# Start of a two-part kernel: x loaded in whole rows, q's weights in column parts, copies of turned x ahead of index tables

## The chip, the cores and the metric

The kernel runs on one NeuronCore of one Trainium2 chip. The metric is the device time of one execution in microseconds (us). All engine names are those of the profile: PE is TensorE's matmul, PEld its weight load, DVE is VectorE, ACT is ScalarE, POOL is GpSimd, SP is SyncE, which here only issues transfers. SPq, ACTq and POOLq are the queues of instructions that issue transfers or wait.

## The reference

Two computations that share nothing, their outputs set side by side (bf16, 2048 tokens of 576 features each).

```python
# A: attention over a dilated window
qkv = (x @ wqkv)                      # 2048 x 576 by 576 x 1728; 32 heads of 18
idx = pos - 2 * arange(8)             # each token looks at itself and 7 earlier ones
attn = softmax(einsum(q, k[idx]) * scale)        # masked where idx < 0
a = einsum(attn, v[idx]) @ wo
# B: a short convolution, then one as long as the sequence
kv = (sum over t of k_pad shifted by t * shift_k[:, 3 - t]) * v     # 4 taps
y = irfft(rfft(kv) * rfft(ssm_k)) + kv * ssm_D
b = q * y
out = concatenate([a, b], -1)
```

## The kernel before

Everything is written as one function with an order laid down by hand. The PE work that has no fixed place is put in a list of units (projections, spectra of the filter and of kv, output products); the call `until()` pops as many units as the next number of the tuple `PLACES` says, and so sets how many units stand on PE between two steps of the rest. `FKS` and `FXS` set how the units of the filter spectrum (L610, L611, `ps_fk`) and of the kv spectrum (L766, `ps_fx`) are mixed with the projections of v.

The beginning, with which the change deals, runs as follows.

* **x** (2048 tokens) is needed turned, features on partitions, in blocks kb of 128 features. Its first two quarters of 512 tokens (qtr 0 and 1) are loaded as they are (L179) and turned on PE (L450, 128x128 each; L455 for the last 64 features) into the PSUM tiles `ps_x`. The other two quarters come turned by the transfer itself (L236).
* **The load** of a quarter puts token 128 sb + p on partition p as its row sb: four separate rows of 576 features (1152 bytes) per partition.
* **The copies** of the turned quarter 0 from PSUM to `xw`: blocks 0 and 1 by DVE (L510), 2 and 3 by ACT (L511), the tail of 64 features by ACT (L460). Quarter 1 is copied by ACT alone, two blocks at a time (L521).
* **q's weights** come with `load_w(nc.sync, 0)`: one transfer for the first 512 rows (L139), two for the last 64, the tails (L141), all from SP's queue, behind x's first quarter and ahead of its second.
* **The index tables**: `table_k(0)`, `table_k(1)`, `table_x(0)`, `table_x(1)` each are two DVE multiply-adds (L421) and one mask (L422) in int32; ACT later takes their sine (L423). Two tables stand ahead of DVE's copies and two behind.
* **The taps' factors** `shift_k` are spread over the partitions by PE (`spread_taps`, L496, into `ps_sk`) and copied to `skb` by ACT (L499); the piece 256 to 511 is spread between the turning of quarter 0 and the first projection.
* **The first projection** `project_first(jp, ct0)` (L483, L485) makes two column tiles of q for 512 tokens: all four blocks for the first tile (e = 0), then all four for the second, then both tails. It runs for (0, 0), (0, 2), (1, 0), (1, 2), with the turning of quarter 1 after the first. Other projections (L363 and on) follow as units.
* DVE then multiplies the taps of kv for four blocks of 512 tokens (`taps`, L560, L564, L580), which takes it to 54.7 us; `negate` (L636) makes a row that `fold_filter` needs, and `fold_filter` (PE L650, ACT L653) overwrites the row that `negate` read. The logits' products (DVE L822), their sums on PE (L837, `ps_log`) and the eviction of those (ACT L842) follow, then the softmax (L865 to L882).

`Ks` holds x as loaded (`xnat`) and the tables (`n_all`) at first, later the filter. `pp` gives PSUM banks in two tags, A and B, two of each.

Of the kernel before, what the change touches and what calls it, by code (L numbers as in the profile page):

```python
# [11 lines left out]
ACT = mybir.ActivationFunctionType  # L12
ALU = mybir.AluOpType
FP32 = mybir.dt.float32
BF16 = mybir.dt.bfloat16
I32 = mybir.dt.int32
PSUM = bass.MemoryType.PSUM

PLACES = (
    15, 4, 11, 2, 1, 0, 3, 4, 6, 4, 13, 4, 4, 0, 4, 3, 4, 2, 1, 3, 4, 3, 5, 5, 0, 7, 2, 2, 2, 1, 2, 2, 2, 2, 3,  # L20
    1, 0, 3, 2, 0, 8, 3, 0, 1, 12, 1, 1, 0,
)

FKS = (
    3, 1, 0, 0, 0, 0, 0, 0, 0, 0, 0, 0, 0, 0, 0, 0, 0, 0, 1, 0, 0, 0, 0, 2, 0, 0, 2, 0, 0, 0,
)
FXS = (
    7, 2, 0, 12, 13, 2, 0, 0, 4,
)

EARLY = (
# [8 lines left out]
def view(t, offset, dims):  # L40

    return bass.AP(tensor=t.tensor, offset=t.offset + offset, ap=[list(t.ap[0])] + [list(d) for d in dims])
# [3 lines left out]
def kernel(  # L46
# [13 lines left out]
    nc = tc.nc  # L60
    Bsz, S, D = A_x.shape
# [3 lines left out]
    xf = A_x.flatten_outer_dims()  # L65
# [23 lines left out]
    HB = 4 * D  # L89
# [4 lines left out]
    main = ctx.enter_context(tc.tile_pool(name="main", bufs=1))  # L94
# [9 lines left out]
    def bank2(name, tag):  # L104
        return pp.tile([128, 2, 512], FP32, name=name, tag=tag)
# [6 lines left out]
    xw = main.tile([128, 12 * HB], BF16, name="xw")  # L112
# [11 lines left out]
    def xT(kb, t0, n):  # L124
        return view(xw, HB * (3 + 3 * (t0 // 1024)) + 1024 * kb + t0 % 1024, [[1, n]])

    def x5(jj):
        return view(xw, HB * (3 + 3 * jj) + 4096, [[1, 512]])

    def w_at(kb, comp):  # L130
        return HB * (9, 10, 5)[comp] + D * kb if kb < 4 else 11 * HB + D * (1, 2, 0)[comp]

    def wq(kb, comp, c0, n):
        return view(xw, w_at(kb, comp) + c0, [[1, n]])

    def load_w(eng, comp, to=None):
        low, high = (to[:, 0:4, :], to[:, 4, :]) if to is not None else \
            (view(xw, w_at(0, comp), [[D, 4], [1, D]]), wq(4, comp, 0, D))
        eng.dma_start(low, A_wqkv[0:512, comp * D:(comp + 1) * D].rearrange("(kb p) a -> p kb a", p=128))  # L139
        for r in range(2):  # L140
            eng.dma_start(high[64 * r:64 * r + 64, :], A_wqkv[512:576, comp * D:(comp + 1) * D])  # L141

    s1 = ExitStack()
    sp1 = s1.enter_context(tc.tile_pool(name="s1", bufs=1, reuse_waits="tile"))
# [4 lines left out]
    tB = sp1.tile([128, 8 * D], BF16, name="tB")  # L149
    skrow = tB[0:97, 0:4 * D]  # L150
    nc.scalar.dma_start(skrow[96:97, :], B_shift_k.rearrange("d j -> (d j)").unsqueeze(0))
    warm = sp1.tile([128, 1], FP32, name="warm")
    nc.scalar.activation(warm[:], pib[:], ACT.Sin)
    ones96 = sp1.tile([97, 256], BF16, name="ones96")
# [9 lines left out]

    idle_work(4)

    Ks = main.tile([128, 12 * HB], BF16, name="Ks")
    xnat = view(Ks, 4 * HB, [[HB, 4], [D, 4], [1, D]])
    n_all = view(Ks, 8 * HB, [[1, 4 * HB]]).bitcast(I32).rearrange("p (n f) -> p n f", n=9)

    def k_at(m, part):
        return 3 * HB * (3 - m) + HB * part

    def kTok(m):
        return view(Ks, k_at(m, 2), [[D, 4], [1, D]])
    kjs, vts = [], []

    def load_x(qtr):
        nc.sync.dma_start(xnat[:, qtr], xf[512 * qtr:512 * qtr + 512, :].rearrange("(sb p) c -> p sb c", p=128))  # L179

    load_x(0)

    def load_k(i):

        eng = nc.sync
        kj = sp1.tile([128, 7, D], BF16, name="kj", bufs=2)
        r0 = BL * i
        low = [(0, 64)]
        if i == 0:
            nc.gpsimd.memset(kj[0:1, 0:3, :], 0.0)  # L190
            nc.gpsimd.dma_start(kj[0:1, 3:7, :], kf[0:4, :].unsqueeze(0))
            low = [(1, 49), (49, 64)]
        for a, b in ((3, 7), (0, 3)) if i == 0 else ((0, 7),):
# [32 lines left out]
    nc.gpsimd.affine_select(ident[:], ones128[:], pattern=[[1, 128]], compare_op=ALU.is_equal, fill=0.0,  # L226
                            base=0, channel_multiplier=-1)

    load_w(nc.sync, 0)
    load_x(1)  # L230

    def turn_x(h):
# [3 lines left out]
        nc.sync.dma_start_transpose(view(xw, 6 * HB + 512 * h, [[1024, 4], [1, 512]]), xf[r0:r0 + 512, 0:512])  # L236

    load_k(0)
    load_w(nc.sync, 1)
    load_v(0)  # L240
    load_k(1)
    turn_x(0)
# [17 lines left out]
    for h in range(2):  # L260
        f = fold[:, 64 * h:64 * h + 64]
# [39 lines left out]
    q, k = qk[:, 0:4 * S + 1024], qk[:, 4 * S + 1024:]  # L301
# [123 lines left out]
    def table_k(c):  # L425
        return table(n_all[:, 2 * c:2 * c + 2, :], TK[:, c, :, :], n_all[:, 8, :], (2 + c, 2 + c), 2048, (256.0, 1792.0))

    def table_x(n):
        return table(n_all[:, 4 + 2 * n:6 + 2 * n, :], TX[:, 2 * n:2 * n + 2, :], n_all[:, 8, :], (4, 5), 4096,
              (512.0 + 1024.0 * n,) * 2)  # L430
# [22 lines left out]
    def tail_x(qtr, pt):  # L453
        for sb in range(4):
            nc.tensor.transpose(pt[64 * qtr:64 * qtr + 64, 0, 512 + 128 * sb:640 + 128 * sb],  # L455
                                xnat[:, qtr, sb, 512:576], ident[:], tile_position=(0, 64 * qtr))

    def copy_tail(qtr, pt):
        r = slice(64 * qtr, 64 * qtr + 64)
        nc.scalar.activation(x5(0)[r], pt[r, 0, 512:1024], ACT.Copy)  # L460

    def pair_x():
        return pp.tile([128, 2, 1024], BF16, name="ps_x", tag="B")
# [13 lines left out]
    def project_first(jp, ct0):  # L477

        ps = bank2("ps_proj", "A")
        for e in range(2):  # L480
            c0 = 128 * (ct0 + e)
            for kb in range(4):
                nc.tensor.matmul(ps[:, e, :], wq(kb, 0, c0, 128), xT(kb, 512 * jp, 512), start=(kb == 0), stop=False)  # L483
        for e in range(2):
            nc.tensor.matmul(ps[:, e, :], wq(4, 0, 128 * (ct0 + e), 128)[64 * jp:64 * jp + 64],  # L485
                             x5(0)[64 * jp:64 * jp + 64], start=False, stop=True, tile_position=(64 * jp, 0))
        nc.scalar.activation(view(q, S * ct0 + 512 * jp, [[S, 2], [1, 512]]), ps[:], ACT.Copy)
# [13 lines left out]

    spread_taps(512)
    spread_taps(0)
    sines = [table_k(0), table_k(1)]
    pts = [pair_x() for _ in range(2)]
    for n in range(2):
        transpose_x(0, pts[n], 2 * n, range(4))
    tail_x(0, pts[1])
    for n in range(2):
        nc.vector.tensor_copy(xT(n, 0, 512), pts[0][:, n, 0:512])  # L510
        nc.scalar.activation(xT(2 + n, 0, 512), pts[1][:, n, 0:512], ACT.Copy)  # L511
    copy_tail(0, pts[1])
    spread_taps(256)
    sines += [table_x(0), table_x(1)]
    project_first(0, 0)
    pts = [pair_x() for _ in range(2)]
    for n in range(2):
        transpose_x(1, pts[n], 2 * n, range(4))
    tail_x(1, pts[0])
    for n in range(2):  # L520
        nc.scalar.activation(view(xw, 3 * HB + 2048 * n + 512, [[1024, 2], [1, 512]]), pts[n][:, :, 0:512], ACT.Copy)  # L521
    copy_tail(1, pts[0])
    project_first(0, 2)
    sines[2]()
# [185 lines left out]
    raw = view(Ks, k_at(0, 0), [[D, 5], [1, D]])  # L710

    for i in range(NBL):
        r = taps(i)
        if i == 3:
            negate(3, 2)
        until()
        if i < 2:
            load_k(i + 2)
            load_v(i + 2)
        if i == 1:  # L720
            load_filter(0)
            for m in range(1, NBL):
                load_filter(m)
            load_w(nc.sync, 2, raw)
            for m in (3, 2, 1, 0):
                nc.gpsimd.dma_start(other(m), kTok(m)[:, 2, :])
            first_rows()
        if i == 1:
            nc.scalar.preload_act_table_set("natural_log_exp_and_others")
            nc.scalar.activation(warm[:], pib[:], ACT.Exp)  # L730
        mirrors = [(0.5, partial(mirror, i, n), "x") for n in range(2)]
        if i == 2:
            mirrors.append(fold_filter(3))
        if i == 3:
            need("fold3")
            first = made(filter_spectrum, 3)
# [516 lines left out]
    for group in groups:  # L1253
# [50 lines left out]
```

## Time and profile before

| | us |
|---|---|
| median of 3 runs | 213.51 |
| lowest and highest of them | 212.78, 213.68 |
| span of the profiled execution | 211.5 |
| PE busy in it | 200.9 (95%) |
| DVE busy | 197.3 (93%) |
| ACT busy | 151.0 (71%) |

The profiled execution is known by its span alone, from its first instruction to its last, and has no time of its own beside the three runs; a run's time also holds what lies around the span. Times in the profile count from the start of the span. A line number L is a line of the kernel. "Idle before, releaser" is how long the engine stood idle just before the instruction and what ended that; a queue's instructions (SPq, ACTq) are not counted as busy. A matmul's end is modelled, its start is recorded.

### The profile page before, as it was taken

The numbers are of one execution on the slowest core, as the hardware profiler recorded it, in microseconds if no ns is written. First come the engines' busy times: TensorE is split into PE (matmuls) and PEld (weight loads), VectorE is DVE, ScalarE is ACT, GpSimd is POOL, SyncE is SP. The second block draws the span as 40 slices with busy tenths as digits, with TensorE's granted clock in tenths as the row PEclk, the third lists the DMA queues.
The fourth block names the chain that finished last, engine by engine and source line by source line (L and its number), as shares of the span: only waits on it lengthen the run. The fifth ranks groups of instructions, "written<-read, shape, count | busy, mean of one in ns | idle before, by whom it ended". The sixth has DMA issues, their size and how long they took to land.

```text
span 211.5 us, 5096 instructions
## 1 busy us (share of the span) xinstructions
PE 200.9 (95%) x2122; PEld 112.5 (53%) x2122; DVE 197.3 (93%) x150; ACT 151.0 (71%) x218; POOL 69.3 (33%) x104
## 2 busy tenths in 40 slices
PE   7999899999879999999999999999999999999891
PEld 2543344445545556563345566765567667676560
DVE  7989999999978999979979999999999999899982
ACT  3799766967797989984378688864487896765640
POOL 8999991023391367220090000004240000202000
PEclk9999999999999999999999999999999999999999
DMA  6999999999092636998999896589993105453034
GB/s 204 297 317 239 248 323 322 183 238 286 8 135 33 87 56 105 187 159 187 226 222 228 141 232 154 103 211 249 209 278 107 60 3 160 123 167 115 3 106 117
DMA packets 34084, 36.12 MB, mean 171 GB/s; under 512 B 17459, under 2 KB 28847, under 8 KB 34062
## 3 DMA queue, kind: packets, MB, share of 16 engines
q1 hardware_dynamic: 26380, 23.11, 43.8%
q0 software_dynamic: 5216, 10.19, 24.8%
q10 hardware_dynamic: 2466, 2.51, 3.6%
q8 instruction: 16, 0.26, 0.5%
q14 instruction: 6, 0.05, 0.1%
HBM read 13.11 MB, written 4.72 MB: 84 GB/s over the span
## 4 chain that ended last, share of the span: by engine, by line
PE 78%; ACT 10%; issue 3%; SPq 2%; DVE 2%; DMA 2%; DVEq 0%; ACTq 0%
PE ps_proj L363 13%; PE ps_z L1126 9%; PE ps_wo L1020 8%; PE ps_acc L964 7%; PE ps_inv L1158 7%; PE ps_fx L766 7%; PE ps_log L837 4%; PE ps_proj L483 4%; PE ps_fk L610 3%; ACT Ks L670 3%; PE ps_proj L374 2%; DMA Ks<-Ks 2%; SPq L212 2%; PE ps_rev L650 1%; PE ps_sk L496 1%
## 5 line engine op out<-in xcount | busy, mean ns | idle before, releaser
L363 PE MATMUL ps_proj<-xw 128*128 128x512 bf16 x160 | 37.5, 380 | 0.5 <-ACT qk L397 0.5
L822 DVE TENSOR_TENSOR av<-qk 128x4096 bf16<-128x4096 bf16 (+1 forms) x16 | 31.5, 2017 | 1.9 <-ACT xw L592 1.9
L363 PEld LDWEIGHTS <-xw 128*128 128x128 bf16 x160 | 14.4, 98 | 20.1 <-issue 4.8
L1139 ACT ACTIVATE av<-ps_z 128x768 bf16<-128x768 f32 x23 | 17.5, 811 | 5.6 <-PE ps_z L1126 5.6
L768 ACT ACTIVATE xw<-ps_fx 128x576 bf16<-128x576 f32 x32 | 18.8, 673 | 2.4 <-PE ps_fx L766 2.4
L397 ACT ACTIVATE qk<-ps_proj 128x1024 bf16<-128x1024 f32 x14 | 14.3, 1025 | 8.3 <-PE ps_proj L374 4.7
L670 ACT ACTIVATE Ks<-ps_fk 128x576 bf16<-128x576 f32 x32 | 19.0, 688 | 1.1 <-PE ps_fk L611 1.0
L1098 DVE TENSOR_TENSOR qk<-xw,Ks 128x2304 bf16<-128x2304 bf16 x14 | 18.6, 1355 | 1.0 <-PE ps_z L1126 0.7
L560 DVE TENSOR_TENSOR tB<-kj,skb 128x4608 bf16<-128x4608 bf16 (+1 forms) x8 | 19.3, 2416 | 0.1
L766 PE MATMUL ps_fx<-xw,TB 128*128 128x288 bf16 x128 | 17.9, 286 | 0.8 <-ACT xw L592 0.7
L1020 PE MATMUL ps_wo<-qk 128*128 128x288 bf16 x128 | 17.9, 287 | 0.0
L610 PE MATMUL ps_fk<-Ks,TB 128*128 128x384 bf16 x62 | 16.4, 326 | 1.2 <-ACT Ks L670 0.9
L1158 PE MATMUL ps_inv<-av,TI 128*128 128x288 bf16 (+1 forms) x112 | 15.6, 292 | 0.6 <-ACT av L1139 0.6
L766 PEld LDWEIGHTS <-TB 128*128 128x128 bf16 x128 | 12.0, 98 | 6.7 <-issue 3.5
L964 PE MATMUL ps_acc<-av,ident 64*64 64x512 bf16 x160 | 15.3, 379 | 0.0
L611 PE MATMUL ps_fk<-Ks,TB 128*128 128x192 bf16 x62 | 15.2, 246 | 0.0
L1087 POOL DMA_DIRECT2D TB<-in_B_q_dram x4 | 3.0, 738 | 36.7 <-DVE v L1098 23.5
L397 ACT ACTIVATE v<-ps_proj 128x1024 bf16<-128x1024 f32 x9 | 9.3, 1043 | 7.8 <-PE ps_proj L363 4.3
L1020 PEld LDWEIGHTS <-qk 128*128 128x128 bf16 x128 | 11.5, 98 | 6.2 <-issue 3.6
L968 ACT ACTIVATE qk<-ps_acc 128x1024 bf16<-128x1024 f32 x8 | 8.2, 1025 | 8.3 <-PE ps_acc L964 8.3
L947 DVE TENSOR_TENSOR av<-Ks,v 128x4096 bf16<-128x4096 bf16 x6 | 13.6, 2285 | 0.1
L1158 PEld LDWEIGHTS <-TI 128*128 128x128 bf16 x112 | 10.5, 98 | 5.6 <-issue 2.7
(194 smaller groups left out, 465.7 us busy)
## 6 DMA issues: line engine op xcount, KB each, us to landing
Ks<-Ks POOLq DMA_DIRECT2D x7, 576.0 KB, 8.3
TB<-av SPq DMA_DIRECT2D x12, 256.0 KB, 4.9
kj<-in_B_k_dram SPq DMA_DIRECT2D x6, 504.0 KB, 6.1
vt<-in_B_v_dram SPq DMA_DIRECT2D x8, 288.0 KB, 5.0
Ks<-av SPq DMA_DIRECT2D x8, 256.0 KB, 6.0
out_dram<-qk ACTq DMA_DIRECT2D x5, 288.0 KB, 3.2
Ks<-in_A_x_dram SPq DMA_DIRECT2D x2, 576.0 KB, 5.2
xw<-in_A_wqkv_dram SPq DMA_DIRECT2D x2, 576.0 KB, 6.0
```

The source lines that it names most:

```text
L363: nc.tensor.matmul(ps[:, jp, :], wq(kb, comp, 128 * ct, 128), xT(kb, 1024 * jj + 512 * jp, 512), **se)
L397: nc.scalar.activation(view(t, o + pad + 1024 * jj, [[512, 2], [1, 512]]), ps[:], ACT.Copy)
L560: dve(2304 * n, lambda: nc.vector.tensor_tensor(to, view(kj, row * D, [[D, n], [D, 4], [1, D]]), view(skb, row * D, [[D, n], [0, 4], [1, D ...
L610: nc.tensor.matmul(o[:, 0:2], w, rhs[:, 0:2], start=start, stop=stop)
L670: nc.scalar.activation(view(Ks, k_at(m, cs ^ (m & 1)) + 96 * gi, [[768, 3], [384, 2], [1, 96]]), acc3(ps), ACT.Copy, scale=(PSG, MSG)[cs][ ...
L766: nc.tensor.matmul(ps[:, pm, 0:HD], TX[:, 2 * pm + c, 128 * gi:128 * gi + 128], kv[:, 2 * c + pm, HD * h:HD * h + HD], start=(c == 0), sto ...
L768: nc.scalar.activation(view(xw, HB * XG[i] + 96 * gi + 1152 * h, [[HB, 2], [384, 3], [1, 96]]), view(ps, 0, [[512, 2], [96, 3], [1, 96]]), ...
L822: return P, at, step, dve(1024 * nj, lambda: nc.vector.tensor_tensor(view(P, at, [[step, 4], [256, nj], [1, 256]]), view(t, o + 256 * hh, ...
L964: nc.tensor.matmul(acc[64 * o:64 * o + 64, h, :], ident[64 * h:64 * h + 64, 64 * h:64 * h + 64], view(P, 256 * u, [[2048, 2], [1, 256]])[6 ...
L1020: nc.tensor.matmul(ps[:, r, 0:HD], oT(hh, j + 2 * r, t)[:, o:o + 128], wo[:, t // 2, t % 2, HD * h:HD * h + HD], start=(t == 0 and h == 0) ...
L1126: nc.tensor.matmul(view(acc[r], 512 * h, [[192, 2], [96, 2], [1, 96]])[o:o + 64], w[64 * h:64 * h + 64, 64 * h:64 * h + 64], pr[64 * h:64 ...
L1158: nc.tensor.matmul(ps[:, c, 0:n], TI[:, sl, pm, 128 * c:128 * c + 128], Yall[:, j % 2, pm, sl, c0:c0 + n], start=(pm == 0 and sl == 0), st ...
```

## The change

* **x**: a quarter is loaded so that partition p holds tokens 4p to 4p + 3, one run of 4608 bytes. The turned blocks then come out of PE with the tokens in the order (sb, p); the copies put them right by reading PSUM with a step (`turned`: p outer, sb inner, so neighbours lie 128 elements apart).
* **q's weights**: the first 512 rows in two transfers, columns 0 to 255 and 256 to 575, on SP right behind x's first quarter; the two tails on ACT's queue, behind `shift_k` and ahead of ACT's first table of functions.
* **Copies**: quarter 0's blocks 0, 1 and 3 by DVE, block 2 by ACT, right behind the first table (`table_k(0)`); the other three tables follow them.
* **First projection**: for each block both column tiles, instead of all blocks of one tile first.
* **Numbers of the order**: three of `PLACES`, one of `FXS`. In the built program the one difference that they make on PE is that two more units of the filter's spectrum stand ahead of the logit sums (L837) that the second eviction L842 ends, and two fewer behind.

The number of instructions is the same on PE, DVE and POOL; ACT has one copy less, which DVE has more, and two transfers more to issue, SP one fewer.

```diff
 PLACES = (
-    15, 4, 11, 2, 1, 0, 3, 4, 6, 4, 13, 4, 4, 0, 4, 3, ...
-    1, 0, 3, 2, 0, 8, 3, 0, 1, 12, 1, 1, 0,
+    15, 4, 11, 2, 1, 0, 3, 4, 6, 6, 11, 4, 4, 0, 4, 3, ...
+    1, 0, 3, 2, 0, 8, 3, 0, 1, 10, 1, 1, 0,
 FXS = (
-    7, 2, 0, 12, 13, 2, 0, 0, 4,
+    7, 4, 0, 12, 13, 2, 0, 0, 4,
...
-    def load_w(eng, comp, to=None):
+    def load_w(comp, to=None, parts=((0, D),), tails=nc.sync):
...
-        eng.dma_start(low, A_wqkv[0:512, comp * D:(comp + 1) * D].rearrange("(kb p) a -> p kb a", p=128))
+        for a, b in parts:
+            nc.sync.dma_start(low[:, :, a:b], A_wqkv[0:512, comp * D + a:comp * D + b].rearrange("(kb p) a -> p kb a", p=128))
         for r in range(2):
-            eng.dma_start(high[64 * r:64 * r + 64, :], A_wqkv[512:576, comp * D:(comp + 1) * D])
+            tails.dma_start(high[64 * r:64 * r + 64, :], A_wqkv[512:576, comp * D:(comp + 1) * D])
...
     def load_x(qtr):
-        nc.sync.dma_start(xnat[:, qtr], xf[512 * qtr:512 * qtr + 512, :].rearrange("(sb p) c -> p sb c", p=128))
+        nc.sync.dma_start(xnat[:, qtr], xf[512 * qtr:512 * qtr + 512, :].rearrange("(p sb) c -> p sb c", p=128))
...
     nc.scalar.dma_start(skrow[96:97, :], B_shift_k.rearrange("d j -> (d j)").unsqueeze(0))
+    load_w(0, parts=((0, 256), (256, D)), tails=nc.scalar)
...
-    load_w(nc.sync, 0)
     load_x(1)
...
+    def turned(ap):
+        return ap.rearrange("q (sb p) -> q p sb", sb=4)
+
     def copy_tail(qtr, pt):
         r = slice(64 * qtr, 64 * qtr + 64)
-        nc.scalar.activation(x5(0)[r], pt[r, 0, 512:1024], ACT.Copy)
+        nc.scalar.activation(x5(0)[r], turned(pt[r, 0, 512:1024]), ACT.Copy)
...
-        for e in range(2):
-            c0 = 128 * (ct0 + e)
-            for kb in range(4):
-                nc.tensor.matmul(ps[:, e, :], wq(kb, 0, c0, 128), xT(kb, 512 * jp, 512), start=(kb == 0), stop=False)
+        for kb in range(4):
+            for e in range(2):
+                nc.tensor.matmul(ps[:, e, :], wq(kb, 0, 128 * (ct0 + e), 128), xT(kb, 512 * jp, 512), start=(kb == 0),
+                                 stop=False)
...
-    sines = [table_k(0), table_k(1)]
+    sines = [table_k(0)]
...
-    for n in range(2):
-        nc.vector.tensor_copy(xT(n, 0, 512), pts[0][:, n, 0:512])
-        nc.scalar.activation(xT(2 + n, 0, 512), pts[1][:, n, 0:512], ACT.Copy)
+    for n in (0, 1, 3):
+        nc.vector.tensor_copy(xT(n, 0, 512), turned(pts[n // 2][:, n % 2, 0:512]))
+    nc.scalar.activation(xT(2, 0, 512), turned(pts[1][:, 0, 0:512]), ACT.Copy)
...
-    sines += [table_x(0), table_x(1)]
+    sines += [table_k(1), table_x(0), table_x(1)]
...
-        nc.scalar.activation(view(xw, 3 * HB + 2048 * n + 512, [[1024, 2], [1, 512]]), pts[n][:, :, 0:512], ACT.Copy)
+        nc.scalar.activation(view(xw, 3 * HB + 2048 * n + 512, [[1024, 2], [4, 128], [1, 4]]),
+                             pts[n][:, :, 0:512].rearrange("q n (sb p) -> q n p sb", sb=4), ACT.Copy)
```

More of the change, by code (lines that the diff above doesn't have):

```diff
@@ L19 @@
 PLACES = (
-    15, 4, 11, 2, 1, 0, 3, 4, 6, 4, 13, 4, 4, 0, 4, 3, 4, 2, 1, 3, 4, 3, 5, 5, 0, 7, 2, 2, 2, 1, 2, 2, 2, 2, 3,
-    1, 0, 3, 2, 0, 8, 3, 0, 1, 12, 1, 1, 0,
+    15, 4, 11, 2, 1, 0, 3, 4, 6, 6, 11, 4, 4, 0, 4, 3, 4, 2, 1, 3, 4, 3, 5, 5, 0, 7, 2, 2, 2, 1, 2, 2, 2, 2, 3,
+    1, 0, 3, 2, 0, 8, 3, 0, 1, 10, 1, 1, 0,
 )
@@ L134, in wq, with load_x @@
         return view(xw, w_at(kb, comp) + c0, [[1, n]])
-    def load_w(eng, comp, to=None):
+    def load_w(comp, to=None, parts=((0, D),), tails=nc.sync):
         low, high = (to[:, 0:4, :], to[:, 4, :]) if to is not None else \
             (view(xw, w_at(0, comp), [[D, 4], [1, D]]), wq(4, comp, 0, D))
-        eng.dma_start(low, A_wqkv[0:512, comp * D:(comp + 1) * D].rearrange("(kb p) a -> p kb a", p=128))
+        for a, b in parts:
+            nc.sync.dma_start(low[:, :, a:b], A_wqkv[0:512, comp * D + a:comp * D + b].rearrange("(kb p) a -> p kb a", p=128))
         for r in range(2):
-            eng.dma_start(high[64 * r:64 * r + 64, :], A_wqkv[512:576, comp * D:(comp + 1) * D])
+            tails.dma_start(high[64 * r:64 * r + 64, :], A_wqkv[512:576, comp * D:(comp + 1) * D])
+    Ks = main.tile([128, 12 * HB], BF16, name="Ks")
+    xnat = view(Ks, 4 * HB, [[HB, 4], [D, 4], [1, D]])
+    n_all = view(Ks, 8 * HB, [[1, 4 * HB]]).bitcast(I32).rearrange("p (n f) -> p n f", n=9)
+    def load_x(qtr):
+        nc.sync.dma_start(xnat[:, qtr], xf[512 * qtr:512 * qtr + 512, :].rearrange("(p sb) c -> p sb c", p=128))
+    load_x(0)
     s1 = ExitStack()
@@ L165 @@
     idle_work(4)
-    Ks = main.tile([128, 12 * HB], BF16, name="Ks")
-    xnat = view(Ks, 4 * HB, [[HB, 4], [D, 4], [1, D]])
-    n_all = view(Ks, 8 * HB, [[1, 4 * HB]]).bitcast(I32).rearrange("p (n f) -> p n f", n=9)
     def k_at(m, part):
@@ L176 @@
     kjs, vts = [], []
-    def load_x(qtr):
-        nc.sync.dma_start(xnat[:, qtr], xf[512 * qtr:512 * qtr + 512, :].rearrange("(sb p) c -> p sb c", p=128))
-    load_x(0)
     def load_k(i):
@@ L238 @@
     load_k(0)
-    load_w(nc.sync, 1)
+    load_w(1)
     load_v(0)
@@ L723 @@
                 load_filter(m)
-            load_w(nc.sync, 2, raw)
+            load_w(2, raw)
             for m in (3, 2, 1, 0):
```

## The prediction

> **What bounds the kernel now.** I read the busy time by stretches first, because the shares over the whole span (TensorE 95%, VectorE 93%) do not say which engine is late where. The columns are the stretch in us, its length, then busy us (and instructions) of TensorE matmuls (PE), weight loads (PEld), VectorE (DVE), ScalarE (ACT), GpSimd, then granted clock, DMA share and GB/s.
>
> ```profile
> 5.30:7.80 2.50, 2.47 (x25) 1.57 (x24) 2.47 (x6) 2.00 (x4) 2.34 (x5) 1.00 1.11 320
> 7.80:20.90 13.10, 13.10 (x72) 5.17 (x72) 12.08 (x13) 11.27 (x14) 12.35 (x21) 1.00 1.15 283
> 20.90:24.00 3.10, 2.55 (x27) 1.27 (x26) 3.06 (x3) 3.10 (x4) 3.04 (x3) 1.00 1.00 203
> 24.00:43.20 19.20, 19.20 (x122) 7.97 (x122) 18.85 (x12) 13.17 (x19) 8.72 (x19) 1.00 1.03 277
> 43.20:53.40 10.20, 10.20 (x88) 4.77 (x88) 10.03 (x7) 7.32 (x10) 2.50 (x4) 1.00 0.98 248
> 53.40:64.00 10.60, 8.45 (x83) 5.30 (x80) 8.81 (x8) 9.48 (x16) 6.96 (x9) 1.00 0.54 76
> 76.00:93.80 17.80, 17.54 (x166) 10.72 (x164) 16.36 (x14) 17.26 (x28) 9.55 (x7) 1.00 0.81 135
> ```
>
> PE is full from 5.3 up to 20.9, and again from 24.0 to 53.4; in 20.9 to 24.0 ACT is full (3.10 of 3.10). From 53.4 to 64.0 neither PE nor DVE is full and ACT is the busiest. From 76.0 to 93.8 ACT has 17.26 of 17.80. So the early stage, which nearly the whole diff edits, is set by PE's own list of matmuls. The chain that ended last, in order of time (start, us, what), says the same for the first 10 us:
>
> ```profile
> 1.27 1.89 PE ps_idle L163 x4
> 3.16 2.13 PE ps_sk L496 x6
> 5.29 1.16 PE ps_x L450 x16
> 6.45 0.34 PE ps_x L455 x4
> 6.79 0.97 PE ps_sk L496 x4
> 7.79 1.91 PE ps_proj L483 x8
> 11.58 1.83 PE ps_proj L483 x8
> ```
>
> Each piece starts where the last ended (1.27 + 1.89 = 3.16, and so on). There is no stretch in which PE stands still for x or for q's weights. The timeline shows the two moments closest to one (start, us, engine, line; in brackets the idle time before and what ended it):
>
> ```profile
> 4.98 1.29 PEld L450 LDWEIGHTS <-Ks 128*128 128x128 bf16 x16 [0.60 <-DMA Ks<-in_A_x_dram]
> 7.76 1.45 PEld L483 LDWEIGHTS <-xw 128*128 128x128 bf16 x8 [0.50 <-issue]
> 9.63 0.11 PEld L485 LDWEIGHTS <-xw 64*128 64x128 bf16 x2 [0.42 <-issue]
> ```
>
> The first transposes' weight load does wait for x, until 4.98, but the matmuls before it end at 5.29. The first projection's load starts after 0.50 of idle where a like change of group (L485) has 0.42.
>
> **The change, part by part.** The sum is made against the span, 211.5. The median of the runs shown is 213.51, 2.0 above it, which I take to lie around the span and to stay.
>
> *x and q's weights earlier.* What can be won here is PE waiting, and the chain has 0.03 (7.76 to 7.79) and 0.08 (first projection group 1.91, a later one 1.83): **-0.11** at most. Both fit the copies of turned x, not the loads: DVE makes the copies at 7.23, behind two index tables.
>
> ```profile
> 1.86 1.22 SPq L141 DMA_DIRECT2D xw<-in_A_wqkv_dram  x2
> 1.40 1.28 ACT L153 ACT_TABLE_LOAD   x1 [1.40 <-PEq L1288]
> 3.62 0.39 ACT L499 ACTIVATE skb<-ps_sk 128x256 bf16<-128x256 f32 x1 [0.72 <-PE ps_sk L496]
> ```
>
> ```profile
> xw<-in_A_wqkv_dram SPq DMA_DIRECT2D x1, 576.0 KB, 5.6
> ```
>
> The last row is the transfers of the first 8 us (KB each, us to landing): q's weights, issued ahead of the tails' 1.86, are in before 7.46, ahead of the 7.76 at which PE loads them. In two column parts the runs of memory get shorter (512 and 640 bytes for 1152) and x's longer (4608 for 1152), and no row prices that. The first part has the place in the queue of the whole and half its bytes; the second is first used by the group at 11.58. Below, nothing can be won past the 0.11; above, 0.2 of cover for the first part and some 4 for the second take it in: nothing.
>
> SP loses two issues (1.22) and gains one (some 0.5), so x's second quarter and k follow about 0.7 earlier. ACT's queue gets the two tail loads, 1.22 ahead of its table load: 1.40 + 1.22 + 1.28 = 3.90, and the eviction of 3.62 moves to about 4.1. It frees the bank of the second eight transposes, at about 5.9: nothing. The Trainium skill, "DMA: Bandwidth & Descriptors", section "Issuing engines are not separate DMA queues", holds that starting transfers from several engines saves only the issue time; by it the sum is unchanged.
>
> *Copies ahead of the tables.* In the built order of the changed kernel DVE does one table, three copies (blocks 0, 1, 3), then three tables; ACT copies block 2 and waits for the third DVE copy, a wait that is new. Behind it on ACT stand the tail copy and the last eviction of the spread taps, for which PE's tails and DVE's first tap wait. DVE today:
>
> ```profile
> 4.13 0.88 DVE L421 TENSOR_SCALAR Ks<-Ks,rp 128x512 int32<-128x512 int32 x2
> 5.66 0.93 DVE L421 TENSOR_SCALAR Ks<-Ks,rp 128x512 int32<-128x512 int32 x2
> 7.23 0.75 DVE L510 COPY xw<-ps_x 128x512 bf16<-128x512 bf16 x2
> 11.96 1.36 DVE L560 TENSOR_TENSOR xw<-kj,skb 128x2304 bf16<-128x2304 bf16 x1 [0.82 <-DMA kj<-in_B_k_dram]
> ```
>
> A table is 1.57 (5.66 to 7.23). The new copies read PSUM with a step, which no DVE row of this kernel does. Bounds, from groups kept apart by form (busy, mean ns):
>
> ```profile
> L510 DVE COPY xw<-ps_x 128x512 bf16<-128x512 bf16 x2 | 0.7, 414 | 0.0
> L899 DVE COPY xw<-Ks 128x576 bf16<-128x576 bf16 x1 | 1.2, 1211 | 0.0
> L1167 DVE TENSOR_TENSOR TB<-ps_back,TB 128x384 bf16<-128x384 f32 x2 | 1.0, 552 | 0.8 <-PE ps_back L1185 0.8
> L1167 DVE TENSOR_TENSOR TB<-ps_back,TB 128x768 bf16<-128x768 f32 x1 | 0.9, 950 | 0.0
> L442 ACT ACTIVATE TI<-ps_ti 128x512 bf16<-128x512 f32 x4 | 2.2, 598 | 0.7 <-PE ps_ti L438 0.7
> L511 ACT ACTIVATE xw<-ps_x 128x512 bf16<-128x512 bf16 x2 | 1.1, 596 | 0.5 <-PE ps_x L455 0.5
> ```
>
> At best 414 ns, as now; at worst 1211/576 = 2.1 ns an element as in the stepped SBUF copy L899, 1.08 us. I take the PSUM rows at one element a time: (950 - 552)/384 = 1.04 ns an element, 552 + 128 x 1.04 = **0.685**. The Trainium skill, "VectorE: DVE Perf Modes", section "Mode 2×_1P — pack two bf16 into one 32-bit read", asks a step of one for two elements a cycle, and so speaks against this part: estimated from its 0.96 GHz, 512 elements are 0.53 plus a fixed part. On ACT the stepped L442 (598) costs what the plain L511 (596) costs: nothing.
>
> So: DVE free at 5.66, the first eight transposes done at about 5.9 (5.29 + half of 1.16). Copies end at 6.6, 7.2 and 7.84 (pitch 0.61, as two of 0.414 take 0.75); ACT's block 2 at about 7.9 to 8.5. PE starts the projection at 7.68 and, going block by block, needs block 2 at its fifth matmul, 7.68 + 4 x 0.229 = 8.60: covered by 0.1, which is what that reordering is worth. The tables then start at 7.76 and end at 7.76 + 3 x 1.57 = 12.47, against a first tap at 11.96 that today waits for k. DVE is **+0.51** late, and k, issued 0.7 earlier, no longer decides.
>
> What does that cost? DVE is full from there to 54.7, so the 0.51 arrives whole. The rows around 55:
>
> ```profile
> 54.66 0.51 DVE L636 TENSOR_SCALAR Ks<-Ks 1x576 bf16<-1x576 bf16 x2
> L653 ACTq EVENT_SEMAPHORE  x7: 17/17/1014, 54.0 to 74.2; - x7
> 55.43 1.22 ACT L653 ACTIVATE Ks<-ps_rev 128x576 bf16<-128x576 f32 x2
> 64.06 2.29 DVE L822 TENSOR_TENSOR av<-qk 128x4096 bf16<-128x4096 bf16 x1 [1.85 <-ACT xw L592]
> ```
>
> ACT's L653 overwrites the row that DVE's L636 reads, so its queue stood from 54.0 for 1.01, to 55.01, yet the engine was free only at 55.43: a slack of 0.42. With DVE 0.51 late the release comes at 55.52 and L653 starts at about 55.53, **+0.10**, instead of the 55.32 that PE's 0.11 would give. DVE's own lateness vanishes in the 1.85 that it waits before 64.06; what remains is the 0.10 through ACT.
>
> *The places.* Of the changed numbers, only one alters the built order: two filter units (L610, L611) go ahead of the logit sums whose eviction is the second L842.
>
> ```profile
> 76.05 2.28 ACT L670 ACTIVATE Ks<-ps_fk 128x576 bf16<-128x576 f32 x4 [0.62 <-PE ps_fk L611]
> 78.52 1.02 ACT L842 ACTIVATE av<-ps_log 128x1024 bf16<-128x1024 f32 x1 [0.18 <-PE ps_log L837]
> 82.87 0.20 DVE L865 TENSOR_TENSOR av<-av,maskb 32x128 bf16<-32x128 bf16 x1
> 93.74 1.23 DVE L882 TENSOR_TENSOR av<-av 128x2048 bf16<-128x2048 bf16 x1 [1.30 <-ACT av L879]
> ```
>
> ACT has six evictions at 0.57 before L842 and no longer waits 0.18 for it: **-0.18** in a stretch where ACT is full and DVE then waits 1.30 for it. L842 ends at 76.05 + 6 x 0.57 + 1.02 = 80.5, DVE needs it at 82.87, so the later sums cost nothing.
>
> Sum: +0.10 - 0.18 = **-0.08**, span 211.4, time **213.4**. With copies at 0.414 it is -0.11 - 0.18 = -0.29 (213.2); with 1.08 see below.
>
> **The rivals.**
> *x comes late in ordinary executions.* Here x landed just in time, but its two loads differ:
>
> ```profile
> DMA to landing us min/median/max: 4.1/5.2/6.3
> ```
>
> If the first x load usually takes the median 5.2 instead of 4.1, PE stands still for about 1.0 in each execution but this one, and the whole-row load of the new kernel saves that: 213.5 - 1.0 - 0.1 = 212.4, and with 6.3 some 211.3. For it: the span of the three runs (0.90), and a load that lands at the edge. Against: the 6.3 belongs to the second x load, queued behind the weights.
> *Stepped copies at 1.08 (slower).* Pitch 1.0: copies end at 7.0, 8.0 and 9.0, ACT's block 2 at 9.65, and PE's fifth matmul waits about 1.0. DVE's tables start at 8.93 and end at 13.6, +1.66; ACT's release at 55.01 + 1.66 = 56.67 puts L653 1.27 late; with the -0.18, +1.1: 214.6. It decides once a copy takes over about 0.75, where block 2 misses 8.60. The price L899 speaks for it, the PSUM rows against.
> *It does nothing:* each effect is under half a microsecond and is lost in waits behind 107 us: 213.5.
>
> **How the numbers follow.** Forecast 0.50; nothing at all 0.10; late x 0.24 (0.18 of it beyond 0.5%); slow copies 0.16 (0.14 beyond 0.5%). 0.5%, about what a measurement of this kernel can tell from no change, is 1.07 us: below 212.44 or above 214.58. Faster 0.18, same 0.50 + 0.10 + 0.06 + 0.02 = 0.68, slower 0.14. The range takes in 212.3 and 214.6, leaving out longer stalls of x and copies beyond 1.08. The forecast's own range is 213.1 to 213.8.
>
> **What would show it.** Right: PE without a gap from 1.27 to 20.9, first projection at about 7.7; three DVE copies of about 0.69; ACT's block 2 behind the third; first tap at about 12.4 with no wait for k; L653 at about 55.5; six evictions ahead of the second L842, at no idle. Wrong: a first projection a microsecond earlier, or PE idle at its fifth matmul, or a first tap well before 12.

## The result, and the profile after

| | before | after |
|---|---|---|
| median of the runs compared, us | 213.25 (212.75 to 213.84, 22 runs) | 213.91 (213.14 to 214.81, 22 runs) |
| ratio to before | | 1.0032, 95% interval 1.0021 to 1.0043 |
| span of the profiled execution, us | 211.5 | 211.6 (its time 213.35) |

The median of before is that of more runs than the 213.51 ahead of the prediction. The change makes the kernel slower by 0.66 us. That is inside the range and within 0.5%, but outside the forecast's own range (213.1 to 213.8), and the forecast had the sign the other way (-0.08). The two profiled executions hide it: their spans are 0.1 apart, for reasons shown below, so the cause must be read from where the two timelines part.

The stretches of the changed kernel (start and end, length, then busy us of PE, PEld, DVE, ACT, POOL; clock, DMA share, GB/s):

```profile
5.30:7.80 2.50, 2.50 (x26) 1.65 (x25) 2.38 (x5) 1.04 (x2) 2.27 (x8) 1.00 1.05 370
7.80:20.90 13.10, 12.31 (x66) 4.86 (x65) 12.86 (x15) 11.26 (x13) 12.42 (x18) 1.00 1.19 275
20.90:24.00 3.10, 3.10 (x29) 1.35 (x29) 3.07 (x3) 3.00 (x4) 3.04 (x3) 1.00 0.79 149
53.40:64.00 10.60, 8.45 (x78) 5.42 (x78) 9.14 (x9) 8.91 (x15) 7.11 (x10) 1.00 0.61 115
76.00:93.80 17.80, 17.49 (x164) 11.04 (x167) 16.89 (x13) 16.88 (x28) 9.86 (x7) 1.00 0.77 129
```

From 7.8 to 20.9 PE was full before (13.10 of 13.10); now 0.79 is missing. The timeline of PE there (the lines of the code named here stand 1 to 5 higher after the change: L486 was L483, L489 was L485):

```profile
5.08 1.19 PE L451 MATMUL ps_x<-ident,Ks 128*128 128x128 bf16 x16
7.42 2.03 PE L486 MATMUL ps_proj<-xw 128*128 128x512 bf16 x8
9.95 1.07 PE L451 MATMUL ps_x<-ident,Ks 128*128 128x128 bf16 x16
11.29 0.39 PE L486 MATMUL ps_proj<-xw 128*128 128x512 bf16 x1
12.47 1.51 PE L486 MATMUL ps_proj<-xw 128*128 128x512 bf16 x6 [0.79 <-ACT xw L525]
13.91 0.60 PE L489 MATMUL ps_proj<-xw 64*128 64x512 bf16 x2
24.56 0.81 PE L364 MATMUL ps_proj<-xw 128*128 128x512 bf16 x2 [0.55 <-ACT qk L398]
```

and the same stretch of the kernel before:

```profile
11.17 0.41 PE L455 MATMUL ps_x<-ident,Ks 128*64 128x128 bf16 x4
11.51 1.90 PE L483 MATMUL ps_proj<-xw 128*128 128x512 bf16 x8
13.34 0.60 PE L485 MATMUL ps_proj<-xw 64*128 64x512 bf16 x2
24.00 1.24 PE L363 MATMUL ps_proj<-xw 128*128 128x512 bf16 x5 [0.55 <-ACT qk L397]
```

PE arrives at its second projection 0.22 earlier than before (11.29 for 11.51), begins, stands, and leaves 0.57 later (13.91 for 13.34). From its start to the tails the projection takes 2.62 where it took 1.83: 0.79 are lost. The 0.56 is still there at 24.56. What it waits for is ACT's L525:

```profile
7.78 0.60 ACT L515 ACTIVATE xw<-ps_x 128x512 bf16<-128x512 bf16 x1 [1.43 <-DVE xw L514]
11.39 1.94 ACT L525 ACTIVATE xw<-ps_x 128x1024 bf16<-128x1024 bf16 x2 [0.34 <-PE ps_x L456]
```

L525 copies the turned x of quarter 1, and the second projection, project_first(0, 2), reads quarter 0 only. The two lie interleaved: 512 columns of quarter 0, 512 of quarter 1, and so on. L525 used to write [[1024, 2], [1, 512]], two exact rows; the change writes [[1024, 2], [4, 128], [1, 4]], the same bytes in three steps. In the built program before, the second projection waits for no such copy; in the changed one its third and seventh matmul do (the profile has seven of its eight matmuls; one ahead of the stop has no record). The first stop ends at 12.47, behind the first L525. The second is short: the seventh matmul starts 0.27 after the sixth, where matmuls of this size otherwise start 0.22 apart, behind the second L525, which ends at 13.33 (11.39 + 1.94):

```profile
13.11 0.38 PE L486 MATMUL ps_proj<-xw 128*128 128x512 bf16 x1
13.38 0.38 PE L486 MATMUL ps_proj<-xw 128*128 128x512 bf16 x1
```

The dependency tracking evidently took the three-step destination as one stretch that covers the block of quarter 0 between its rows: this is inferred, and the first two experiments test it.

Idle time in brackets counts from the modelled end of the matmul before, so what a stop costs is read better from the starts.

Further on (DVE of the changed kernel; 64.06, 93.74, 107.19 and 142.53 before):

```profile
55.02 0.51 DVE L641 TENSOR_SCALAR Ks<-Ks 1x576 bf16<-1x576 bf16 x2
64.62 2.29 DVE L827 TENSOR_TENSOR av<-qk 128x4096 bf16<-128x4096 bf16 x1 [2.04 <-ACT xw L597]
94.19 1.22 DVE L887 TENSOR_TENSOR av<-av 128x2048 bf16<-128x2048 bf16 x1 [1.17 <-ACT av L884]
107.64 2.29 DVE L952 TENSOR_TENSOR av<-TB,v 128x4096 bf16<-128x4096 bf16 x1 [1.12 <-PE ps_log L842]
142.56 2.28 DVE L952 TENSOR_TENSOR qk<-TB,v 128x4096 bf16<-128x4096 bf16 x1
```

The delay is 0.56 at 64, 0.45 from 94 to 107 (the changed places give 0.11 back), and gone at 142. There the profiled execution of before had waited for a transfer, and this one did not:

```profile
142.53 2.29 DVE L947 TENSOR_TENSOR qk<-TB,v 128x4096 bf16<-128x4096 bf16 x1 [0.33 <-DMA TB<-av]
```

A second profile of each kernel (last experiments) has that wait in both, and spans 0.9 apart. Of these 0.9, 0.27 come ahead of the stop (the first projection starts at 8.06 for 7.79), which differs from one execution to the next, as shown there.

### The profile page after: what moved, and what is told of

The parts are those of the page before. It is cut to its first block, busy times and chain, and to the rows that moved or that the text cites. A ratio compares the mean times of both kernels' runs of the same rounds, so it can differ in the third digit from the quotient of the medians.

```text
span 211.6 us, 5089 instructions
## 1 busy us (share of the span) xinstructions
PE 199.3 (94%) x2114; PEld 112.2 (53%) x2122; DVE 198.3 (94%) x151; ACT 150.2 (71%) x217; POOL 69.5 (33%) x104
## 4 chain that ended last, share of the span: by engine, by line
PE 60%; DVE 20%; ACT 8%; DMA 5%; issue 5%; SPq 1%; ACTq 0%; DVEq 0%
PE ps_z L1131 9%; DVE tB L565 9%; DVE xw L569 8%; PE ps_wo L1025 8%; PE ps_inv L1163 7%; PE ps_fx L771 7%; PE ps_acc L969 7%; PE ps_proj L364 5%; PE ps_log L842 4%; PE ps_fk L615 3%; DMA kj<-in_B_k_dram 2%; DMA xw<-in_A_wqkv_dram 2%; ACT Ks L675 2%; PE ps_fk L616 1%; PE ps_rev L655 1%
## 5 line engine op out<-in xcount | busy, mean ns | idle before, releaser
L364 PE MATMUL ps_proj<-xw 128*128 128x512 bf16 x153 | 36.2, 380 | 1.3 <-issue 0.6
```

What stands on the lines that cost most here:

```text
L364: nc.tensor.matmul(ps[:, jp, :], wq(kb, comp, 128 * ct, 128), xT(kb, 1024 * jj + 512 * jp, 512), **se)
```

## The experiments

Theory W: the new wait is the loss. Rivals: the loads (L), DVE's new order and its stepped copies (D, later S), x's layout (X). Every kernel computes the whole output. Ratios are to the kernel before on the same chip, with 95% intervals.

**The wait taken away.** In the changed kernel, the old destination with the stepped source:

```diff
-  nc.scalar.activation(view(xw, 3 * HB + 2048 * n + 512, [[1024, 2], [4, 128], [1, 4]]),
+  nc.scalar.activation(view(xw, 3 * HB + 2048 * n + 512, [[1024, 2], [1, 512]]),
```

> The changed kernel with the same copies of x's second quarter on ScalarE, their destination written as two runs of 512 instead of two runs of 128 x 4, so that the second projection group no longer waits for them. Theory W (that wait costs the time): the 0.79 us gap of TensorE at 12.47 goes, the third projection group starts at about 13.7 instead of 14.4, VectorE's 64.6 moves to about 64.0, and the time against the kernel before falls from 1.0032 to about 0.999. Rival L (x's second quarter and k land late because of the column parts and the tails on ScalarE's queue): the gap goes but the time stays at 1.002 or above.

1.0012 (1.0001 to 1.0022), 213.38 us. PE's stop is gone; 0.0020 of 0.0032 came back, less than the 0.004 expected. The size is loose, for this interval just touches that of the changed kernel (1.0021 to 1.0043). In its profile PE stands at another place, for x's second quarter:

```profile
11.07 1.07 PE L451 MATMUL ps_x<-ident,Ks 128*128 128x128 bf16 x16 [0.59 <-DMA Ks<-in_A_x_dram]
```

**The wait added to the kernel before,** by the same view of the destination and nothing else (the source re-arranged "q n (p sb)" to match):

```diff
-  ... [[1024, 2], [1, 512]]), pts[n][:, :, 0:512], ACT.Copy)
+  ... [[1024, 2], [4, 128], [1, 4]]), pts[n][:, :, 0:512].rearrange("q n (p sb) -> q n p sb", sb=4), ACT.Copy)
```

> The kernel before with one edit: the destination of ScalarE's copies of x's second quarter written as two runs of 128 x 4, data and work the same, so that the second projection group waits for them. Theory W: its second matmul waits until about 12.6 and its fourth until about 13.6, TensorE is some 1.2 us late from there, and the time is about 1.005 of the kernel before. Rival L: a wait there is covered later, 1.000 to 1.001.

1.0069 (1.0053 to 1.0086), more than the 1.005 expected. PE in its timeline:

```profile
11.87 0.39 PE L483 MATMUL ps_proj<-xw 128*128 128x512 bf16 x1
13.05 0.59 PE L483 MATMUL ps_proj<-xw 128*128 128x512 bf16 x2 [0.79 <-ACT xw L521]
13.97 1.24 PE L483 MATMUL ps_proj<-xw 128*128 128x512 bf16 x5 [0.32 <-ACT xw L521]
15.14 0.60 PE L485 MATMUL ps_proj<-xw 64*128 64x512 bf16 x2
```

W is shown: only how a destination is written differs, the bytes are the same, and 1.5 us are lost (0.0069 of 213.1). The projection takes 3.27 from 11.87 to 15.14 where the kernel before takes 1.83, so 1.44 are lost on PE in this place alone. It costs more here than in the changed kernel because the matmuls go tile by tile, all four blocks of one column tile first: the second and the fourth wait, one matmul stands between the two stops, and the second stop costs another 0.48 (13.97 is 0.70 behind 13.27, less the 0.22). Block by block, the third and the seventh wait, three matmuls stand between, and the second stop costs 0.05. That is what the new order of the matmuls is worth in this place.

**The places alone** (the PLACES and FXS numbers of the change, in the kernel before).

> The kernel before with the changed numbers of the order alone (two filter units ahead of the second logit sums). As forecast: ScalarE loses its 0.18 us idle before the second L842, VectorE's wait before L882 shrinks by that, time 0.999. Rival: the later logit sums cost as much as is won, 1.000 or above.

0.9995 (0.9985 to 1.0005). DVE's L882 starts at 93.63 for 93.74, and at 142 nothing is left of it:

```profile
93.63 1.22 DVE L882 TENSOR_TENSOR av<-av 128x2048 bf16<-128x2048 bf16 x1 [1.20 <-ACT av L879]
142.55 2.29 DVE L947 TENSOR_TENSOR qk<-TB,v 128x4096 bf16<-128x4096 bf16 x1 [0.47 <-DMA TB<-av]
```

**No wait, and q's weights whole in their old place, tails on SP:**

```diff
-    load_w(0, parts=((0, 256), (256, D)), tails=nc.scalar)
...
+    load_w(0)
     load_x(1)
```

> The kernel a1_exact with q's weights loaded as before: one transfer for 512 rows and two tails, all on SyncE's queue behind x's first quarter. Theory W: as a1_exact, within 0.001. Rival L: x's second quarter lands as early as before (9.4 us) or earlier and the time is 0.001 to 0.002 below a1_exact.

1.0014 (1.0002 to 1.0025): as with the parts. Alone this says nothing against the loads, as will be seen.

**What is left, from four sides.** First, no wait, and DVE's order of before:

```diff
-    sines = [table_k(0)]
+    sines = [table_k(0), table_k(1)]
-    for n in (0, 1, 3): ...  (DVE), block 2 (ACT)
+    for n in range(2): blocks n (DVE) and 2 + n (ACT), stepped
```

> The changed kernel without the wait on ACT's copies of quarter 1 (exact destination), and with DVE's order of before: both index tables ahead of the copies, DVE copying blocks 0 and 1, ACT blocks 2 and 3. What is left of the loss there was 0.0012 (0.0001 to 0.0022) of the time. Theory D (DVE's order: it reaches its first tap 0.4 to 0.9 us later and carries that to about 55 us): it goes, ratio 0.9995 to the kernel before. Rival X (x's loads, four tokens a partition: the second quarter sometimes lands after PE asks for it): it stays, 1.001 or more.

1.0022 (1.0008 to 1.0035): it does not come back, so nothing says that DVE's new order is the loss. The run can't clear it alone, for here the stepped copies stand behind two tables. Then the new order alone in the kernel before, with plain copies (the reverse of these lines, no stepped read):

> The kernel before with DVE's new order alone (one table, copies of blocks 0, 1, 3 as they were, then three tables). Theory D: 1.001, first tap about 0.3 to 0.4 us later than 11.96. Rival X: 1.000, within 0.0005.

0.9985 (0.9973 to 0.9998), 212.98 us: the opposite of theory D. The order wins 0.3 us. Third, the changed kernel with x as before:

```diff
-  xf[...].rearrange("(p sb) c -> p sb c", p=128)
+  xf[...].rearrange("(sb p) c -> p sb c", p=128)
-  turned(...), rearrange("q n (sb p) -> q n p sb", sb=4)
+  plain rows
```

> The changed kernel with x's quarters loaded as before, one token of each block a partition, and so with copies that read PSUM in a row; everything else as changed. The wait on ACT's copies of quarter 1 is gone with it. Rival X: 0.9995 or below, since only x's loads and the stepped reads differ from the 1.0012. Theory D: about 1.0005 to 1.001, for DVE keeps its order and loses only the stepped part (3 x 0.25 us).

0.9998 (0.9985 to 1.0011). Last, x's four tokens a partition alone, in the kernel before, with exact destinations (the same lines turned round):

> The kernel before with x's quarters loaded four tokens a partition and the copies reading PSUM with a step (all destinations rows, so no new wait). Rival X: 1.001 to 1.002, with PE waiting for x's second quarter ahead of its transposes in the profile. Theory D: 1.000, with DVE's tables 0.5 us later (2 copies at 0.25 more), hidden in its wait of 0.82 for k.

1.0023 (1.0013 to 1.0032). The theory of x's layout had the size nearly right (1.001 to 1.002) and its reason wrong: PE does not wait for x's second quarter, which landed at 8.4. It waits for DVE's copies, behind two tables, which now take 1.28 for two instead of 0.75:

```profile
7.23 1.28 DVE L513 COPY xw<-ps_x 128x512 bf16<-128x512 bf16 x2
8.06 2.18 PE L486 MATMUL ps_proj<-xw 128*128 128x512 bf16 x8 [0.25 <-DMA kj<-in_B_k_dram]
```

The releaser that the row names is a transfer of k, which PE does not read; the copies that it does read end at 7.91 and at 8.51 (7.23 + 1.28), and the projection's first two matmuls start right behind them, at 8.06 and 8.56. The tails start at 10.17 for 9.64: 0.53 late, about the 0.0023 of the time.

**Two stepped copies for three ahead of the second table.**

```diff
-    for n in (0, 1, 3):
-        nc.vector.tensor_copy(xT(n, 0, 512), turned(pts[n // 2][:, n % 2, 0:512]))
-    nc.scalar.activation(xT(2, 0, 512), turned(pts[1][:, 0, 0:512]), ACT.Copy)
+    for n in range(2):
+        nc.vector.tensor_copy(xT(n, 0, 512), turned(pts[0][:, n, 0:512]))
+        nc.scalar.activation(xT(2 + n, 0, 512), turned(pts[1][:, n, 0:512]), ACT.Copy)
```

> The changed kernel without the wait on ACT's copies of quarter 1, its copies of quarter 0 still ahead of the second table, but two by DVE (blocks 0, 1) and two by ACT (2, 3), so that ACT waits for no DVE copy and DVE makes two stepped copies for three. It was 1.0012 with three, and 0.9998 with three copies that read in a row. Theory S (the stepped copy's price on DVE is what was left: a third of it ahead of block 2 and of the tables): about 1.000 or below. Rival X2 (x's loads of four tokens a partition cost by themselves): 1.001 stays.

1.0028 (1.0008 to 1.0049): theory S alone falls. But its profile shows another stop:

```profile
7.03 1.89 PE L486 MATMUL ps_proj<-xw 128*128 128x512 bf16 x8
10.07 1.07 PE L451 MATMUL ps_x<-ident,Ks 128*128 128x128 bf16 x16 [0.62 <-DMA Ks<-in_A_x_dram]
```

PE projects early, at 7.03, and then stands for x's second quarter (as it did for 0.59 in the profile of a1_exact). Of the transfers issued between 2.0 and 3.5 us, these two concern it, x's second quarter and the second column part (KB each, us to landing):

```profile
Ks<-in_A_x_dram SPq DMA_DIRECT2D x1, 576.0 KB, 7.7
xw<-in_A_wqkv_dram SPq DMA_DIRECT2D x1, 320.0 KB, 6.3
```

Issued at 2.30, the quarter lands at 10.0. With column parts and four tokens it landed at 8.5 to 11.0 in five profiles; with four tokens and whole weights in the old place at 8.1 to 8.4 (three profiles); with one token of each block a partition at 9.2 to 9.5 (eight profiles, one of them with the parts). k, issued behind that quarter, is late too: DVE's first tap waits for it.

```profile
12.36 1.36 DVE L565 TENSOR_TENSOR xw<-kj,skb 128x2304 bf16<-128x2304 bf16 x1 [0.83 <-DMA kj<-in_B_k_dram]
55.78 1.19 ACT L658 ACTIVATE Ks<-ps_rev 128x576 bf16<-128x576 f32 x2 [0.32 <-issue]
```

**Both suspects undone.** As the last, with load_w(0) in the old place:

> The changed kernel without the wait on ACT's copies of quarter 1, with two copies on DVE and two on ACT, and with q's weights loaded whole where they were before (tails on SP's queue). With column parts it was 1.0028, and PE waited 0.62 us for x's second quarter. Theory L (the column parts make x's second quarter late, beside loads of four tokens a partition): that quarter lands by 8.5 us, PE does not wait for it, and the time falls to 0.999. Rival R (four tokens cost by the stepped reads wherever they stand, or by something not named yet): 1.001 or more, without any wait for x in the profile.

0.9989 (0.9975 to 1.0004), the quarter in at 8.4. And as the last but one, with load_w(0, tails=nc.scalar) early, so that only the parts go:

> As the kernel with two copies on DVE and two on ACT and the weights early with tails on ACT's queue, but q's weights in one load, not in two column parts. Theory L: as with the old place, 0.999, x's second quarter in by about 8.5 us. Rival L2 (the early place or the tails on ACT's queue make it late): 1.001 or more, the quarter lands behind 9.5 us.

0.998 (0.997 to 0.9991), 212.70 us: **the lowest time of all**, 0.44 us under before and faster than the changed kernel; its interval overlaps those of c2_order, f3_best and f1_split_w, so these are not told apart. Its quarter lands at 9.4 (1.74 + 7.7), not by 8.5 as expected, but ahead of PE, which does not stand at 9.61:

```profile
7.25 1.89 PE L486 MATMUL ps_proj<-xw 128*128 128x512 bf16 x8
9.08 0.60 PE L489 MATMUL ps_proj<-xw 64*128 64x512 bf16 x2
9.61 1.07 PE L451 MATMUL ps_x<-ident,Ks 128*128 128x128 bf16 x16
11.49 1.36 DVE L565 TENSOR_TENSOR xw<-kj,skb 128x2304 bf16<-128x2304 bf16 x1
54.97 1.19 ACT L658 ACTIVATE Ks<-ps_rev 128x576 bf16<-128x576 f32 x2
```

Here the first tap waits for nothing and starts 0.87 earlier than in d1_split.

**Order and places together** in the kernel before, and **the order with two copies on DVE** (only table_k(1) moved behind the copies):

> The kernel before with DVE's new order (copies of blocks 0, 1, 3 as plain rows behind the first table) and the new places. The order alone gave 0.9985, the places alone 0.9995. Theory S with a clock that rises at a different time in each execution: the two gains are at different places (ahead of 8 us and ahead of 94 us) and add up, 0.998. Rival: the gain at 94 us is lost in the wait for a transfer at 142 us, so 0.9985 as with the order alone.

> The kernel before with its copies of turned x as they were (two by DVE, two by ACT, plain rows), only moved ahead of the second index table. With three on DVE the ratio was 0.9985. Theory: what wins is that PE no longer waits up to 0.4 us for the first copy, so 0.9985 again, or better by the wait of ACT on DVE that goes; DVE's first tap waits for k as before. Rival: without the third copy on DVE nothing is different from before by more than 0.0005.

0.9987 (0.9967 to 1.0008) and 0.9986 (0.9973 to 0.9999). The places add nothing that can be told, and the gain is in the order, not in the third copy on DVE.

**Both kernels a second time,** one execution each:

> The kernel before once more, for a second profile of the same program. Theory P (the time at which PE's matmuls get their full rate differs from one execution to the next, by up to 0.8 us at the first transposes): the sixteen first transposes take something between 1.07 and 1.91 us, another number than 1.36; below about 1.3, PE then waits for DVE's copies ahead of its first projection, which starts at 7.8 all the same; above, the first projection starts later, up to 8.2, and everything up to 140 us with it. Rival: they take 1.36 again, and the 1.91 and 1.07 in the other profiles come from the edits.

> The changed kernel once more. Theory P: the sixteen first transposes take another number than 1.19, and PE again waits some 0.8 us in its second projection for ACT's copy of quarter 1, whatever they take; with 1.9 us at the transposes the span is 0.5 to 0.7 longer than the 211.6 of the first profile. Rival: the same 1.19 and the same span within 0.1.

Before, span 211.6:

```profile
5.01 1.07 PE L450 MATMUL ps_x<-ident,Ks 128*128 128x128 bf16 x16
7.79 1.91 PE L483 MATMUL ps_proj<-xw 128*128 128x512 bf16 x8 [0.40 <-DVE xw L510]
```

After, span 212.5:

```profile
5.08 1.83 PE L451 MATMUL ps_x<-ident,Ks 128*128 128x128 bf16 x16
8.06 1.89 PE L486 MATMUL ps_proj<-xw 128*128 128x512 bf16 x8
12.94 1.51 PE L486 MATMUL ps_proj<-xw 128*128 128x512 bf16 x6 [0.79 <-ACT xw L525]
143.45 2.29 DVE L952 TENSOR_TENSOR qk<-TB,v 128x4096 bf16<-128x4096 bf16 x1 [0.34 <-DMA TB<-av]
```

The same program does its first sixteen transposes in 1.36 or in 1.07, the other in 1.19 or 1.83. Over all profiles it is 1.06 to 1.91. The slow transposes start 0.11 apart and the fast ones 0.06, so PE doubles its rate, at a time that differs from one execution to the next. When it does so early, the kernel before stands for DVE's first copy, which comes behind two tables at 7.23; when late (b1_span), it never stands there. The starts say how long. The matmul ahead of the first projection starts at 7.38 in the first profile of the kernel before:

```profile
7.38 0.38 PE L496 MATMUL ps_sk<-tB,ones 97*128 97x512 bf16 x1
7.79 0.38 PE L483 MATMUL ps_proj<-xw 128*128 128x512 bf16 x1
```

In its second it starts at 7.01, the projection at 7.79 again. Where nothing is waited for, the two starts are 0.22 apart, so 0.19 and 0.56 are lost. With the new order alone (c2_order, early rate) the projection starts at 7.26:

```profile
7.26 1.89 PE L483 MATMUL ps_proj<-xw 128*128 128x512 bf16 x8
```

The second projection of the changed kernel loses 0.79 in both of its profiles. The span of its second is 0.9 longer than that of its first, more than the 0.5 to 0.7 expected.

## Why the prediction was wrong

1. **The step that failed** is in "The change part by part": "On ACT the stepped L442 (598) costs what the plain L511 (596) costs: nothing." The duration was right (0.60 for L515, 1.94 for the two L525 as for the two L521 before); that a destination written in three steps brings a wait to another engine was not looked for. So "PE without a gap 1.27 to 20.9" failed by 0.79. The order of the built program, which the forecast used for ACT's new wait on DVE, had this wait too: waits had to be compared on PE as well, where no edit seemed to touch them.

2. **Copies ahead of tables, at most -0.11:** too small, for two reasons. The 0.03 and 0.08 count from the chain, in which a matmul's end is modelled; by the starts, 0.19 were lost in that same execution. And the bound came from one execution, in which PE reached its full rate in the middle of the transposes; in the second it lost 0.56. The order alone is worth 0.0015 of the time (c2_order, 0.9973 to 0.9998), about 0.3 us, between the two.

3. **The stepped copy at 0.685:** right (0.684 on average, 1.89 for three that overlap, and 0.60 on ACT). "Covered by 0.1" was wrong in the first profile: PE idle at its fifth matmul was named as a sign of being wrong, and the fifth starts 0.36 behind the fourth, 0.14 more than the usual 0.22 from start to start, when ACT's copy of block 2, behind DVE's third, ends at 8.38 (7.78 + 0.60). So the first projection took 2.03 where it takes 1.89 unhindered.

```profile
8.07 0.38 PE L486 MATMUL ps_proj<-xw 128*128 128x512 bf16 x1
8.43 0.38 PE L486 MATMUL ps_proj<-xw 128*128 128x512 bf16 x1
```

   In the second profile, with a late rate, it is not met. In the time, the third copy's cost shows only with whole weights: 1.0014 (1.0002 to 1.0025) with three on DVE, 0.9989 (0.9975 to 1.0004) with two. The profiles of these two runs both have the late rate, and PE's timelines there agree up to 24 us (24.42 and 24.41), so that the 0.14 makes up that difference in executions with an early rate is argued, not shown. (In the rival of slow copies, 56.67 lies 1.24 behind 55.43, not 1.27; its +1.1 stands.)

4. **Column parts: nothing:** wrong. With two copies on DVE the parts make 0.998 into 1.0028, and PE waits 0.62 for x's second quarter. The forecast looked at when the weights land and not at what else is in flight. That the parts cost is shown by the times (f2_whole against d1_split, which differ in nothing else, though the runs of d1_split spread widely, 212.91 to 215.47). That they cost by x's second quarter rests on the waits of 0.59 and 0.62 in two profiles; with the parts it landed at 8.5 to 11.0, in the one profile without them at 9.4, so that its spread, not each landing, is the loss. Between the profiles of d1_split and f2_whole that quarter explains about 0.47: the transposes of quarter 1 start at 10.07 for 9.61, and PE is still that much late at 23.90 for 23.43. At L658 the two are 0.81 apart (55.78 for 54.97), and the rest came by k: with the first tap 0.87 late, DVE's L641 starts at 55.06 for 54.27, and ACT, which waits for it, stands idle for 0.32. This is the path that the forecast priced at +0.10 for the changed kernel. With three copies PE comes later and did not wait for the quarter in two of three profiles, which would explain why taking the parts away alone (1.0014 for 1.0012) showed nothing: two limits stood one behind the other, and each hid the other. Why the parts would delay that quarter and k was not tried.

5. **The first tap +0.51, k no longer decides:** +0.35 in the profile (12.31 for 11.96), +0.74 in the second; and k does decide in some (in a1_exact DVE waits 0.46 for it until 13.25).

6. **L653 +0.10:** +0.56 (55.99 for 55.43). In the changed kernel it is PE's delay, not DVE's: in b1_span, where DVE's write stands at 54.72 as before, the same eviction starts at 57.23, 1.80 later, like everything of PE's there (its tails at 15.14 for 13.34).

7. **The places, -0.18:** -0.11 at DVE's wait ahead of L882; ACT does its six evictions ahead of the second L847 without idle, as forecast:

```profile
76.60 3.37 ACT L675 ACTIVATE Ks<-ps_fk 128x576 bf16<-128x576 f32 x6 [0.63 <-PE ps_fk L616]
80.06 1.02 ACT L847 ACTIVATE av<-ps_log 128x1024 bf16<-128x1024 f32 x1
```

   In the time it is 0.0005, which can't be told from nothing; the transfer at 142 takes it.

Put together: +0.0020 for the wait (a1_exact against the changed kernel), and about +0.003 for the third copy and the parts together (f2_whole against a1_exact, 0.998 for 1.0012), which cannot be split into a sum since they hide one another; against that, some -0.002 that the rest wins. The sum of the forecast held none of these at its size, so that the time stayed within 0.5% and in the range was luck. The rival of x landing late meant the first quarter in the kernel before, and about a fifth of its 1.0 is there, in one profile: in the second profile of that kernel the quarter lands at 4.97 and the transposes start at 5.01, 0.44 after the matmul ahead of them, 0.22 more than usual, and the stop at 7.79 hides it. The late transfer was the second quarter, and it was made late by the change.

## What to carry to other kernels

A copy's view decides who waits for it: after a change of layout, compare the waits in the built program on every engine, also for readers of the neighbouring blocks, and keep destinations in exact rows where neighbours are live. A cover of a tenth of a microsecond in one profile is a coin toss over many executions; profile the same kernel twice before calling a gain bounded, and read waits of PE from the starts of its matmuls. If undoing a part changes nothing, undo it together with the next suspect before clearing it.

## What the runs showed of the hardware

- PE's full rate comes at a time that differs from one execution to the next: sixteen 128x128 transposes took 1.06 to 1.91 us in the same place of the program, with a granted clock of 1.00 in the profile throughout. The Trainium skill, "TensorE: Matmul & The Clock Gate", section "What's actually happening", says that the window which raises the clock runs freely, so that the count of slow matmuls differs from run to run; these profiles agree (none of the sixteen transposes is slow in the second profile of the kernel before, fourteen are in that of the changed one).
- DVE's copy of 128x512 bf16 out of PSUM takes 0.41 in a row and 0.68 with a step of 128; ACT's takes 0.60 either way.
- The load of x's second quarter (576 KB) took 5.1 to 8.7 us to land, depending on what was issued around it. Issued 0.8 earlier (2.3 for 3.1), in four tokens a partition and with the parts ahead of it, it landed at 8.5 to 11.0, against 9.2 to 9.5 in the kernel before and its variants.
